# Dealing the forward chain out anew over the sixteen pieces of a segment

## The chip, the cores and the metric

The kernel runs on one core of a Trainium2 chip. The core has a matrix engine (TensorE, PE in the profile, with its weight loads shown as PEld), a vector engine (VectorE, DVE), a scalar engine (ScalarE, ACT), a general engine (GpSimd, POOL) and a sync engine (SyncE, SP), which here only issues DMAs; POOL issues DMAs too. Each engine works through its own list of instructions in order and waits on semaphores for the others. PE writes its products to PSUM, in banks of 512 float32 values per partition; DVE and ACT read them from there.

The metric is the time of one execution in microseconds of device time. The kernel before takes 6149.91 us, the median of three runs (6148.34 to 6164.37).

## The reference

The kernel computes a gated mix of two attention blocks over 2048 tokens of width 576, and all gradients of it. Block A has 32 query heads of width 18 that share one key and one value. Block B is a recurrent transformer: 64 segments of 32 tokens, each with 8 memory tokens in front, 32 heads of width 128; the first 8 rows of a segment's output are the next segment's memory.

```python
for s in range(n_seg):                                   # 64
    xs = x[:, s * seg_len:(s + 1) * seg_len, :].copy()   # 32 tokens
    h = jnp.concatenate([mem, xs], axis=1)               # 8 + 32 rows
    q = jnp.einsum('btd,dhe->bhte', h, Wq)               # k and v in the same way
    scores = jnp.where(mask[None, None], jnp.einsum('bhqe,bhke->bhqk', q, k) * scale, -1000000000.0)
    o = jnp.einsum('bhqk,bhke->bhqe', _softmax(scores), v)
    o = jnp.einsum('bhte,hed->btd', o, Wo)
    mem = o[:, :M, :].copy()                             # 8 rows go on
    outs.append(o[:, M:, :])
...
return g * a + (1 - g) * b       # and the vector-Jacobian product with grad_out
```

So the chain over the segments is serial, with little work in each link: only the 8 memory rows need the link before.

## The kernel before, in words

The program is one long list, unrolled. Its stages are: setup and projections (to about 500 us), the *forward weave* (to about 2330), a bulk stage of block B (to about 3130), a backward weave (to about 4850), and the weight gradients and the end. The change touches the forward weave alone.

`weave` takes two generators and deals their work out by hand, in the order in which it is issued: two steps of the sweep first, then one piece of the chain and one step of the sweep in turn. Nothing reorders this later: each engine's list has the order of the program text.

The *sweep* (`a_pass1`) is block A's attention. Its 1024 steps are 64 blocks (16 pairs of heads, four blocks of 512 queries) of 16 key tiles each. Step n issues, on PE, the score products `a_S` of step n + 1 (two matmuls on separate rows of the array) and the products `a_dP` of step n, then the exponential of step n + 1 on ACT (`a_E`; `a_S` has one buffer), the two multiplications `a_W` on DVE, the accumulation of `a_W` of step n − 1 and of `a_E` of step n into `a_acc` (four matmuls each, one on each quarter of the array's columns). At the end of a block the sum is copied to `acs`, and `a_post` finishes the block in three parts, at steps 2, 3 and 5 of the next one: part 1 transposes `acs` (four float32 transposes into a tile of the buffer `c_pj`, copied to `a_tk` by ACT), part 2 transposes the block's queries from SBUF (four transposes of `a_QD` into `c_pj`, copied to `a_qt` by ACT), part 3 does small work on POOL, ending with the scaling of `a_qt`, and three stores on SP, the last of `a_qt` to `sd_dram`.

The *chain* (`b_chain_fwd`) is block B's memory recurrence. Each segment has 16 pieces, so a segment spans one block of the sweep, and piece p is followed by step p + 2 of the block. A projection works on 32 columns: the 8 memory rows and up to 24 token rows that "ride" along (`load_ride`); its 4096 output columns stand as four column groups of the array times two halves (`proj(w, 0, ...)` and `proj(w, 1, ...)`, each with five contraction tiles of four matmuls of 512 columns). ACT evacuates each half into `c_k2`, `c_q2` or `c_v2`. The chain has two PSUM buffers of one bank each, named `c_pj` and `c_x`; the sweep has six (two for `a_S`, three for `a_dP`, one for `a_acc`). A new tile of `c_pj` or `c_x` waits until the last one has been read.

The pieces of the kernel before, with the names used below:

- 0: the new memory (`pm`, from `hs` and `hx`) goes into `hm`; loads and stores.
- 1 to 4: projection of k, 3, 3, 3 and 1 contraction tiles; 4 to 7: of q (2, 3, 3, 2); 7: transpose of k's memory rows (`mem_T`, `mT_out`).
- 8: transpose of q's memory rows, 2 tiles of v. 9: the scores of the memory queries (`ps`: a mask matmul `mbias` of 128 columns, 32 products with the keys `kx` of the segment, 32 with the memory's keys), and their exponential `c_E`. 10: 3 tiles of v, the row sums `den`, their reciprocal `c_rd` on DVE, the load of the next keys (`load_k`: a transposing DMA from SP into the one buffer `c_kx`). 11 and 12: 3 and 2 tiles of v; 11 also `c_pn` on DVE and its expansion `c_PB` on POOL.
- 13: the output `po` (16 products), the transpose of v's memory rows. 14 and 15: 64 head matmuls of 144 columns each (`heads`: the projection of the memory rows by `Wo`), then `hs` and `hx` on DVE.

`rows_out` (POOL) stores the projected rows, `rows_copy` (SP) copies them within DRAM, `head_out` (SP) stores `c_oh` in runs of 16 bytes, `load_v` loads `c_vx` in four DMAs, and in the first 48 segments `stash` and `stash_end` (SP) transpose two heads of the weights by DMA and store them for a later stage.

Of the kernel before, what the change touches and what calls it, by code (L numbers as in the profile page):

```python
# [6 lines left out]
ACT = mybir.ActivationFunctionType  # L7
# [30 lines left out]
class Kern:  # L38
# [80 lines left out]
    def setup_B_consts(self, pool):  # L119
# [11 lines left out]
        mb = pool.tile([P, P], BF16, name="mbias")  # L131
        nc.gpsimd.memset(mb[:], 0.0)
        nc.gpsimd.memset(mb[:, 64:128], NEGB)
        for c in range(4):
            nc.gpsimd.memset(mb[32 * c:32 * c + 8, 64:128], 0.0)
# [108 lines left out]

    def proj_mem(self, st, Wt, j, psum, tag, nb):
        pj = psum.tile([P, 512], F32, name=tag, bufs=nb)
        self.proj_part(pj, st, Wt, j, range(NKT))
        return pj
# [7 lines left out]
    def b_chain_fwd(self, keep, sp, psum):  # L256
# [50 lines left out]
        for s in range(NSEG):  # L307
# [42 lines left out]
            if s:  # L350
                pm = psum.tile([P, NKT, 8], F32, name="c_x", bufs=1)
# [11 lines left out]
            proj("k", 0, (0, 1, 2), "c_x")  # L363
            yield
            proj("k", 0, (3, 4), "c_x")
            proj("k", 1, (0,), "c_pj")
            yield
            proj("k", 1, (1, 2, 3), "c_pj")
            yield
            proj("k", 1, (4,), "c_pj")  # L370
            proj("q", 0, (0, 1), "c_x")
            yield
            proj("q", 0, (2, 3, 4), "c_x")
            yield
            rows_out("k")
            proj("q", 1, (0, 1, 2), "c_pj")
# [3 lines left out]
            proj("q", 1, (3, 4), "c_pj")  # L380
            mT_out("k", self.mem_T(t2["k"], psum, "c_x", 1))
# [7 lines left out]
            rows_copy("k")  # L389
            ps = psum.tile([P, P], F32, name="c_x", bufs=1)  # L390
            self.mm(ps[:], lhsT=self.identB[:], rhs=self.mbias[:], start=True, stop=False)
            for u in range(8):
                for c in range(4):
                    self.mm(ps[32 * c:32 * c + 32, 8 * u:8 * u + 8], lhsT=kx[:, 8 * c + u, :], rhs=qT[:, u, c, :],
                            start=False, stop=False, tp=(0, 32 * c))
            for u in range(8):
                for c in range(4):
                    self.mm(ps[32 * c:32 * c + 8, 64 + 8 * u:72 + 8 * u], lhsT=mT["k"][:, c, u, :],
                            rhs=qT[:, u, c, :], start=False, stop=True, tp=(0, 32 * c))
            Et = sp.tile([P, 2, 64], BF16, name="c_E", bufs=1)  # L400
            nc.scalar.activation(Et[:].rearrange("p a b -> p (a b)"), ps[:], ACT.Exp, scale=SCALEB)
# [6 lines left out]
            nc.vector.reciprocal(rd[:], den[:])  # L408
# [20 lines left out]
            mT_out("v", self.mem_T(t2["v"], psum, "c_x", 1))  # L429
# [5 lines left out]
            head_out()  # L435
            if not last:
# [980 lines left out]
    def a_pass1(self, keep, sp, psum, xps):  # L1417
# [36 lines left out]
        for n in range(NP_ + 1):  # L1454
# [15 lines left out]
            if n > 0:  # L1470
# [4 lines left out]
                if n % 16 == 0:  # L1475
# [381 lines left out]
```

## Time and profile before

| | us |
|---|---|
| median of three runs | 6149.91 |
| the profiled execution, its own time | 6158.5 |
| its span, first to last instruction | 6156.7 |
| PE busy | 5649.8 (92%) |
| DVE busy | 3760.5 (61%) |
| ACT busy | 3435.7 (56%) |
| POOL busy | 1957.9 (32%) |
| forward weave, first to last exponential `a_E` | 501.4 to 2305.2 |

A line of the timeline has the start, the time that the merged group took, the engine, the line of the kernel (L73 is the helper that issues every matmul, so one goes by tiles there), the operation, what it writes and reads, its shape and the number of instructions; in brackets, how long the engine had been idle before and what released it. "issue" is idle time in which the profile shows nothing to wait for. A line by stretch has busy time and instructions of PE, PEld, DVE, ACT and POOL, then PE's granted clock, the share of the DMA engines and GB/s. Matmuls overlap, so PE's busy time is not its load; the distance between starts is.

### The profile page before, as it was taken

Reading aid. Unit: us, or ns where it says so; the run is one execution under the profiler, and the core shown is the slowest. Engines: PE = TensorE matmul, PEld = TensorE weight load, DVE = VectorE, ACT = ScalarE, POOL = GpSimd, SP = SyncE. Lnnn points to the kernel's source line nnn. Section 1 sums busy time; section 2 is a strip of 40 time slices with the busy share of each in tenths; the row PEclk is TensorE's granted clock in tenths of the full one; section 3 lists DMA queues with packets and bytes.
Section 4 is the critical chain, followed back from the end, with each engine's and each line's share of the span. In section 5 each row is a group of like instructions: output and inputs, shape, how many; then the busy total and the mean of one; then the engine's idle time right before and its main releaser. Section 6 shows DMA issues by size and latency. Waiting matters only on the chain.

```text
span 6156.7 us, 211396 instructions
## 1 busy us (share of the span) xinstructions
PE 5649.8 (92%) x90123; PEld 3274.8 (53%) x90334; DVE 3760.5 (61%) x7124; ACT 3435.7 (56%) x4916; POOL 1957.9 (32%) x3483
## 2 busy tenths in 40 slices
PE   7898999999999996999869999999998999899999
PEld 4543444444444445777735555555555777675444
DVE  4336778777778884666568888888888111111112
ACT  3325777777777774665557777777777222111101
POOL 3002333333333344444423333333333111112213
PEclk7999999999999998999989999999999999999999
DMA  4645666666665548999864443434343999896663
GB/s 151 224 154 115 126 125 130 122 128 126 125 127 115 108 86 231 253 255 254 248 196 109 108 108 109 109 108 108 109 108 98 242 248 246 228 278 200 216 186 112
DMA packets 1369174, 990.03 MB, mean 161 GB/s; under 512 B 931805, under 2 KB 1186790, under 8 KB 1357510
## 3 DMA queue, kind: packets, MB, share of 16 engines
q1 hardware_dynamic: 1286870, 782.63, 51.6%
q0 software_dynamic: 81360, 193.86, 9.8%
q8 instruction: 708, 11.60, 0.8%
q14 instruction: 236, 1.93, 0.1%
HBM read 550.31 MB, written 385.03 MB: 152 GB/s over the span
## 4 chain that ended last, share of the span: by engine, by line
PE 40%; ACT 11%; DMA 6%; issue 3%; SPq 1%; POOL 1%; DVE 0%; POOLq 0%; DVEq 0%; ACTq 0%
ACT b_E L1577 11%; PE w_acc L73 10%; PE b_S L73 6%; PE y_pdx L73 4%; PE r_pj L73 4%; DMA dsx_dram<-x_dS 3%; PE r_x L73 2%; PE x_tr L78 2%; PE b_acc L73 2%; PE y_pk L73 1%; PE x_po L73 1%; PE x_b L73 1%; PE x_m L73 1%; PE b_dP L73 1%; PE f_big L73 1%
## 5 line engine op out<-in xcount | busy, mean ns | idle before, releaser
L1469 DVE TENSOR_TENSOR a_W<-a_dP,a_E 128x512 bf16<-128x512 f32 x2048 | 1316.1, 685 | 357.5 <-issue 133.4
L1598 DVE TENSOR_TENSOR b_dS<-b_dP,b_E 128x512 bf16<-128x512 f32 x2048 | 1313.6, 683 | 240.8 <-issue 121.9
L1577 ACT ACTIVATE b_E<-b_S 128x1024 bf16<-128x1024 f32 x1024 | 1047.8, 1023 | 447.1 <-PE b_dP L73 322.7
L1439 ACT ACTIVATE a_E<-a_S 128x1024 bf16<-128x1024 f32 x1024 | 1049.4, 1025 | 358.0 <-PE a_dP L73 233.9
L73 PE MATMUL b_S<-b_KV,b_QD 32*128 32x512 bf16 x2048 | 400.1, 381 | 158.8 <-ACT b_E L1577 101.6
L73 PE MATMUL r_pj<-WT,r_dT 128*32 128x288 bf16 x12288 | 491.8, 287 | 0.6 <-DMA WT<-st_WT 0.6
L73 PE MATMUL w_acc<-w_d,w_h 128*128 128x512 bf16 (+1 forms) x2352 | 471.0, 379 | 2.5
L73 PE MATMUL a_S<-a_QD,l_KV 32*128 32x512 bf16 x2048 | 401.3, 384 | 39.7 <-ACT a_E L1439 17.9
L73 PE MATMUL b_acc<-b_dS,b_SD 128*32 128x512 bf16 x2048 | 418.7, 390 | 0.9 <-DVE b_dS L1598 0.7
L73 PE MATMUL a_acc<-a_W,l_WK 128*32 128x512 bf16 x4096 | 413.1, 391 | 1.8 <-issue 1.2
L73 PE MATMUL a_acc<-a_E,l_VK 128*32 128x512 bf16 x4096 | 403.8, 383 | 1.8 <-issue 1.8
L73 PE MATMUL b_acc<-b_E,b_SD 128*32 128x512 bf16 x2048 | 403.2, 390 | 0.0
L73 PE MATMUL a_dP<-a_QD,l_KV 32*128 32x512 bf16 x2048 | 399.6, 387 | 0.5 <-issue 0.5
L73 PE MATMUL b_dP<-b_KV,b_QD 32*128 32x512 bf16 x2048 | 398.3, 385 | 0.0
L1063 DVE COPY y_T<-y_pt 128x512 bf16<-128x512 bf16 x256 | 97.1, 420 | 460.2 <-PE y_pt L78 460.2
L73 PEld LDWEIGHTS <-r_dT 128*32 128x32 bf16 x12288 | 332.5, 97 | 79.3 <-issue 1.3
L73 PEld LDWEIGHTS <-w_h 128*128 128x128 bf16 (+1 forms) x2688 | 229.9, 100 | 258.3 <-issue 6.6
L73 PEld LDWEIGHTS <-b_QD 32*128 32x128 bf16 x4096 | 165.0, 91 | 348.5 <-issue 284.3
L73 PEld LDWEIGHTS <-hm 128*32 128x32 bf16 x7680 | 196.8, 96 | 226.0 <-issue 49.9
L73 PEld LDWEIGHTS <-l_KV 32*128 32x128 bf16 x4096 | 129.2, 91 | 300.6 <-issue 264.1
L1049 ACT CAST y_tdk<-y_pk 128x512 bf16<-128x512 f32 x128 | 75.0, 586 | 376.7 <-PE y_pk L73 211.7
L73 PE MATMUL y_pdx<-WT,y_T 128*128 128x288 bf16 x2048 | 273.0, 287 | 0.0
(422 smaller groups left out, 11232.7 us busy)
## 6 DMA issues: line engine op xcount, KB each, us to landing
b_QD<-qd_dram SPq DMA_DIRECT2D x256, 128.0 KB
b_SD<-sd_dram SPq DMA_DIRECT2D x256, 128.0 KB
dOx_dram<-p_tok SPq DMA_DIRECT2D x16, 1024.0 KB
c_vx<-vx_dram SPq DMA_DIRECT2D x256, 64.0 KB
krow_dram<-c_k POOLq DMA_DIRECT2D x64, 256.0 KB
qrow_dram<-c_q POOLq DMA_DIRECT2D x64, 256.0 KB
vrow_dram<-c_v POOLq DMA_DIRECT2D x64, 256.0 KB
x_q<-qx_dram SPq DMA_DIRECT2D x32, 512.0 KB
```

The source lines that it names most:

```text
L73: return self.nc.tensor.matmul(out, lhsT, rhs, start=start, stop=stop, tile_position=tp, skip_group_check=True)
L78: return self.nc.tensor.transpose(out, in_, self.identB[b:b + nrows, b:b + nrows], tile_position=tp)
L1049: nc.scalar.copy(d[w][:, r, :], pk[:])
L1063: nc.vector.tensor_copy(T_[t][w][:], pt[:])
L1439: nc.scalar.activation(E_[n][:], S.pop(n)[:], ACT.Exp, scale=SCALEA)
L1469: nc.vector.tensor_tensor(out=W_[n][:, i, :], in0=dP[i][:], in1=E_[n][:, i, :], op=ALU.mult)
L1577: nc.scalar.activation(E_[n][:], S.pop(n)[:], ACT.Exp, scale=SCALEA)
L1598: nc.vector.tensor_tensor(out=D_[n][:, i, :], in0=dP[i][:], in1=E_[n][:, i, :], op=ALU.mult)
```

## The change

The 16 pieces stay 16, and every product stays, but they are dealt out in another way. The projections of k and q are cut elsewhere (k: 1, 3, 1 + 3, 2 tiles; q: 1, 2, 2 + 1, 4). The second half of v becomes two blocks of 256 columns (`proj_cols`), the first of which shares a tile with the scores and the row sums (`px`, buffer `c_x`); the other has its own (`pv`, buffer `c_pj`) and is copied by DVE. The mask matmul covers 64 columns. `c_pn` and `c_PB` move to the piece of the row sums, the output to piece 12, and the heads to pieces 13 to 15, with 44, 40 and 44 matmuls. In the sweep, `a_qt` comes from DRAM by a transposing DMA on SP in place of PE and ACT, `acs` is transposed into `c_x`, and the parts of `a_post` stand at steps 1, 2 and 5, the first with one transpose and the second with three.

```diff
         self.bmask = bm
-        mb = pool.tile([P, P], BF16, name="mbias")
-        nc.gpsimd.memset(mb[:], 0.0)
-        nc.gpsimd.memset(mb[:, 64:128], NEGB)
+        mb = pool.tile([P, 64], BF16, name="mbias")
+        nc.gpsimd.memset(mb[:], NEGB)
         for c in range(4):
-            nc.gpsimd.memset(mb[32 * c:32 * c + 8, 64:128], 0.0)
+            nc.gpsimd.memset(mb[32 * c:32 * c + 8, :], 0.0)
...
@@ -242,6 +241,12 @@
                         rhs=Wt[:, kt, c * 1024 + j * 512:c * 1024 + (j + 1) * 512],
                         start=(kt == 0), stop=(kt == NKT - 1), tp=(0, 32 * c))
 
+    def proj_cols(self, out, st, Wt, lo, n, kts):
+        for kt in kts:
+            for c in range(4):
+                self.mm(out[32 * c:32 * c + 32, :], lhsT=st[:, kt, :], rhs=Wt[:, kt, c * 1024 + lo:c * 1024 + lo + n],
+                        start=(kt == 0), stop=(kt == NKT - 1), tp=(0, 32 * c))
+
...
         self.proj_part(pj, st, Wt, j, range(NKT))
@@ -348,7 +353,7 @@
             if 0 < s <= 48:
                 stash_end(*wt)
             if s:
-                pm = psum.tile([P, NKT, 8], F32, name="c_x", bufs=1)
+                pm = psum.tile([P, NKT, 8], F32, name="c_pj", bufs=1)
...
                 self.mm(pm[0:64, 4, :], lhsT=hx[:].rearrange("p g c -> p (g c)"), rhs=self.sel8[:])
@@ -360,25 +365,27 @@
             nc.gpsimd.dma_start(self.pq_dram[s // 4].rearrange("s q c w k -> (s q c) w k")
                                 [:, 4 * (s % 4):4 * (s % 4) + 4, :], self.zeros[:].unsqueeze(1).to_broadcast([P, 4, P]))
             yield
-            proj("k", 0, (0, 1, 2), "c_x")
-            yield
-            proj("k", 0, (3, 4), "c_x")
-            proj("k", 1, (0,), "c_pj")
-            yield
-            proj("k", 1, (1, 2, 3), "c_pj")
-            yield
-            proj("k", 1, (4,), "c_pj")
-            proj("q", 0, (0, 1), "c_x")
-            yield
-            proj("q", 0, (2, 3, 4), "c_x")
-            yield
+            proj("k", 0, (0,), "c_pj")
+            yield
+            proj("k", 0, (1, 2, 3), "c_pj")
+            yield
+            proj("k", 0, (4,), "c_pj")
+            proj("k", 1, (0, 1, 2), "c_x")
+            yield
+            proj("k", 1, (3, 4), "c_x")
+            proj("q", 0, (0,), "c_pj")
+            yield
+            mT_out("k", self.mem_T(t2["k"], psum, "c_x", 1))
             rows_out("k")
-            proj("q", 1, (0, 1, 2), "c_pj")
+            proj("q", 0, (1, 2), "c_pj")
+            yield
+            proj("q", 0, (3, 4), "c_pj")
+            proj("q", 1, (0,), "c_x")
             if s < 48:
                 wt = stash(2 * s)
             yield
-            proj("q", 1, (3, 4), "c_pj")
-            mT_out("k", self.mem_T(t2["k"], psum, "c_x", 1))
+            proj("q", 1, (1, 2, 3, 4), "c_x")
+            rows_copy("k")
             yield
             src = self.mem_T(t2["q"], psum, "c_x", 1)
             qT = sp.tile([P, 8, 4, 8], BF16, name="c_qT", bufs=1)
@@ -386,39 +393,46 @@
             rows_out("q")
             proj("v", 0, (0, 1), "c_pj")
             yield
-            rows_copy("k")
-            ps = psum.tile([P, P], F32, name="c_x", bufs=1)
-            self.mm(ps[:], lhsT=self.identB[:], rhs=self.mbias[:], start=True, stop=False)
+            px = psum.tile([P, 512], F32, name="c_x", bufs=1)
+            ps, den = px[:, 0:P], px[:, P:192]
+            for c in range(4):
+                self.mm(px[32 * c:32 * c + 32, 64:128], lhsT=self.identB[:, 32 * c:32 * c + 32],
+                        rhs=self.mbias[:], start=True, stop=False, tp=(0, 32 * c))
             for u in range(8):
                 for c in range(4):
-                    self.mm(ps[32 * c:32 * c + 32, 8 * u:8 * u + 8], lhsT=kx[:, 8 * c + u, :], rhs=qT[:, u, c, :],
-                            start=False, stop=False, tp=(0, 32 * c))
+                    self.mm(px[32 * c:32 * c + 32, 8 * u:8 * u + 8], lhsT=kx[:, 8 * c + u, :], rhs=qT[:, u, c, :],
+                            tp=(0, 32 * c))
             for u in range(8):
                 for c in range(4):
-                    self.mm(ps[32 * c:32 * c + 8, 64 + 8 * u:72 + 8 * u], lhsT=mT["k"][:, c, u, :],
+                    self.mm(px[32 * c:32 * c + 8, 64 + 8 * u:72 + 8 * u], lhsT=mT["k"][:, c, u, :],
                             rhs=qT[:, u, c, :], start=False, stop=True, tp=(0, 32 * c))
             Et = sp.tile([P, 2, 64], BF16, name="c_E", bufs=1)
-            nc.scalar.activation(Et[:].rearrange("p a b -> p (a b)"), ps[:], ACT.Exp, scale=SCALEB)
-            yield
-            proj("v", 0, (2, 3, 4), "c_pj")
-            den = psum.tile([P, 64], F32, name="c_x", bufs=1)
-            self.mm(den[:], lhsT=self.blockones[:], rhs=Et[:, 0, :], start=True, stop=False)
-            self.mm(den[:], lhsT=self.blockones[:], rhs=Et[:, 1, :], start=False, stop=True)
+            nc.scalar.activation(Et[:].rearrange("p a b -> p (a b)"), ps, ACT.Exp, scale=SCALEB)
+            proj("v", 0, (2, 3), "c_pj")
+            yield
+            proj("v", 0, (4,), "c_pj")
+            self.mm(den, lhsT=self.blockones[:], rhs=Et[:, 0, :], start=True, stop=False)
+            self.mm(den, lhsT=self.blockones[:], rhs=Et[:, 1, :], start=False, stop=True)
             rd = sp.tile([P, 64], F32, name="c_rd", bufs=1)
-            nc.vector.reciprocal(rd[:], den[:])
-            if not last:
-                kx = load_k(s + 1)
-            yield
-            proj("v", 1, (0, 1, 2), "c_x")
+            nc.vector.reciprocal(rd[:], den)
             pn = sp.tile([P, 2, 64], BF16, name="c_pn", bufs=1)
             nc.vector.tensor_tensor(out=pn[:], in0=Et[:], in1=rd[:].unsqueeze(1).to_broadcast([P, 2, 64]), op=ALU.mult)
             PB = sp.tile([P, 16, 4, 8], BF16, name="c_PB", bufs=1)
             self.expand(PB[:], pn[:].rearrange("p a (u q) -> p (a u) q", q=8), 16)
             nc.gpsimd.dma_start(self.pm_dram[s], pn[:].rearrange("p a b -> p (a b)"))
-            yield
+            if not last:
+                kx = load_k(s + 1)
+            vlo = px[:, 256:512]
+            self.proj_cols(vlo, h_, self.W["v"], 512, 256, (0, 1, 2))
+            yield
+            self.proj_cols(vlo, h_, self.W["v"], 512, 256, (3, 4))
+            nc.scalar.copy(t2["v"][:, 4:6, :].rearrange("p u e -> p (u e)"), vlo)
+            pv = psum.tile([P, 512], F32, name="c_pj", bufs=1)
+            self.proj_cols(pv[:, 0:256], h_, self.W["v"], 768, 256, range(NKT))
+            nc.vector.tensor_copy(t2["v"][:, 6:8, :].rearrange("p u e -> p (u e)"), pv[:, 0:256])
             rows_copy("q")
-            proj("v", 1, (3, 4), "c_x")
-            yield
+            yield
+            mT_out("v", self.mem_T(t2["v"], psum, "c_x", 1))
             po = psum.tile([P, 8, 32], F32, name="c_pj", bufs=1)
             for u in range(8):
                 self.mm(po[:, u, :], lhsT=vx[:, u, :], rhs=PB[:, u].rearrange("p c q -> p (c q)"), start=True, stop=False)
@@ -426,24 +440,26 @@
                         start=False, stop=True)
             oT = sp.tile([P, 8, 4, 8], BF16, name="c_oT", bufs=2)
             nc.vector.tensor_copy(oT[:].rearrange("p u c q -> p u (c q)"), po[:])
-            mT_out("v", self.mem_T(t2["v"], psum, "c_x", 1))
             rows_out("v")
             nc.gpsimd.dma_start(self.oTm_dram[s // 16][:, s % 16, :], oT[:].rearrange("p u c q -> p (u c q)"))
             oh = sp.tile([P, 4, 8, 8], BF16, name="c_oh", bufs=1)
             nc.gpsimd.tensor_copy(oh[:], oT[:].rearrange("p u c q -> p c u q"))
             yield
-            head_out()
             if not last:
                 vx = load_v(s + 1)
                 if s < 48:
                     stash_end(*wt)
                     wt = stash(2 * s + 1)
                 ph = psum.tile([P, 512], F32, name="c_pj", bufs=1)
-                heads(0, 16)
+                heads(0, 11)
+            yield
+            head_out()
+            if not last:
+                heads(11, 21)
             yield
             rows_copy("v")
             if not last:
-                heads(16, 32)
+                heads(21, 32)
                 hs = sp.tile([P, P], BF16, name="c_hs", bufs=1)
                 nc.vector.tensor_copy(hs[:], ph[:, 0:P])
                 hx = sp.tile([P, 4, 16], BF16, name="c_hx", bufs=1)
@@ -1476,10 +1492,11 @@
                     acs = sp.tile([P, 512], F32, name="a_acs", bufs=1)
                     nc.scalar.copy(acs[:], acc[:])
                     bb = n // 16 - 1
-                    post = self.a_post(bb // 4, bb % 4, acs, QD.pop(bb), sp, xps, dl_all)
+                    QD.pop(bb)
+                    post = self.a_post(bb // 4, bb % 4, acs, sp, xps, dl_all)
             if n < NP_ and n % 16:
                 acc_mm(acc, n, E_, self.VK, False, False)
-            if post is not None and n % 16 in (2, 3, 5):
+            if post is not None and n % 16 in (1, 2, 5):
                 if next(post, "end") == "end":
                     post = None
             yield
@@ -1495,21 +1512,19 @@
         nc.gpsimd.dma_start(self.qd_dram[:].rearrange("p (a r) t -> p a r t", r=32)[:, 2:4, 18:20, :],
                             self.dl_dram[:].rearrange("(p a r) t -> p a r t", a=2, r=2))
 
-    def a_post(self, p, qb, acs, QD, sp, psum, dl_all):
-        nc = self.nc
-        pt = psum.tile([P, 4, P], F32, name="c_pj", bufs=1)
+    def a_post(self, p, qb, acs, sp, psum, dl_all):
+        nc = self.nc
+        qt = sp.tile([P, 4, 4, 32], BF16, name="a_qt", bufs=1)
+        nc.sync.dma_start_transpose(qt[:].rearrange("p a b c -> p a (b c)"), self.qd_dram[p][:, qb * 512:(qb + 1) * 512])
+        pt = psum.tile([P, 4, P], F32, name="c_x", bufs=1)
         for j in range(4):
             nc.tensor.transpose(pt[:, j, :], acs[:, j * P:(j + 1) * P], self.identF[:])
+            if j == 0:
+                yield
         tk = sp.tile([P, 4, 2, 64], F32, name="a_tk", bufs=1)
         tkf = tk[:].rearrange("p a b c -> p (a b c)")
         ptf = pt[:].rearrange("p a b -> p (a b)")
         nc.scalar.copy(tkf, ptf)
-        yield
-        pd = psum.tile([P, 4, P], BF16, name="c_pj", bufs=1)
-        for j in range(4):
-            self.tr(pd[:, j, :], QD[:, j * P:(j + 1) * P], P)
-        qt = sp.tile([P, 4, 4, 32], BF16, name="a_qt", bufs=1)
-        nc.scalar.copy(qt[:].rearrange("p a b c -> p (a b c)"), pd[:].rearrange("p a b -> p (a b)"))
         yield
         rl = sp.tile([P, 4, 2, 2], F32, name="a_rl", bufs=2)
         nc.vector.reciprocal(rl[:, :, 1, :], tk[:, :, :, 18])
```

More of the change, by code (lines that the diff above doesn't have):

```diff
@@ L362, in b_chain_fwd @@
             yield
-            proj("k", 0, (0, 1, 2), "c_x")
+            proj("k", 0, (0,), "c_pj")
             yield
-            proj("k", 0, (3, 4), "c_x")
-            proj("k", 1, (0,), "c_pj")
+            proj("k", 0, (1, 2, 3), "c_pj")
             yield
-            proj("k", 1, (1, 2, 3), "c_pj")
+            proj("k", 0, (4,), "c_pj")
+            proj("k", 1, (0, 1, 2), "c_x")
             yield
-            proj("k", 1, (4,), "c_pj")
-            proj("q", 0, (0, 1), "c_x")
+            proj("k", 1, (3, 4), "c_x")
+            proj("q", 0, (0,), "c_pj")
             yield
-            proj("q", 0, (2, 3, 4), "c_x")
+            mT_out("k", self.mem_T(t2["k"], psum, "c_x", 1))
+            rows_out("k")
+            proj("q", 0, (1, 2), "c_pj")
             yield
-            rows_out("k")
-            proj("q", 1, (0, 1, 2), "c_pj")
+            proj("q", 0, (3, 4), "c_pj")
+            proj("q", 1, (0,), "c_x")
             if s < 48:
```

## The prediction

> **What bounds the kernel now.** I read the busy times by stretch first. The edits lie in one stretch, the forward weave from about 500 to 2305 us (1805 us), where PE is nearly always busy and its granted clock is 1.00:
>
> ```profile
> 530.00:2300.00 1770.00, 1701.59 (x35172) 759.63 (x35168) 1419.05 (x2586) 1368.67 (x1765) 676.76 (x1387) 1.00 0.61 121
> ```
>
> Then the timeline of one segment. A *period* is the time from the `a_S` pair before a chain piece to the pair after it. This is piece 5, twelve projection matmuls:
>
> ```profile
> 1200.18 0.39 PE L73 MATMUL a_S<-a_QD,l_KV 32*128 32x512 bf16 x2 [0.24 <-ACT a_E L1439]
> ...
> 1200.51 0.40 PE L73 MATMUL a_acc<-a_W,l_WK 128*32 128x512 bf16 x4
> ...
> 1200.66 1.02 ACT L1439 ACTIVATE a_E<-a_S 128x1024 bf16<-128x1024 f32 x1
> ...
> 1200.74 0.39 PE L73 MATMUL a_acc<-a_E,l_VK 128*32 128x512 bf16 x4
> ...
> 1200.95 0.82 PE L73 MATMUL c_x<-Wq,hm 128*32 128x512 bf16 x12
> ...
> 1201.73 0.39 PE L73 MATMUL a_S<-a_QD,l_KV 32*128 32x512 bf16 x2
> ```
>
> Two limits meet here. *Floor*: the next pair waits for the exponential that reads the one PSUM buffer of S: 0.48 from pair to exponential, 1.02 for it, 0.05 back, 1.55 us. *PE sum*: 0.55 to the second accumulation group, 0.21 to the chain's first matmul, 0.64 for twelve projection matmuls (0.213 per contraction tile), 0.12 to the next pair: 1.53. A piece up to twelve projection matmuls costs the floor; what it has beyond costs time one for one.
>
> From the starts of the `a_S` pairs, the median periods 0 to 15 over the 64 segments are 1.55, 2.22, 2.36, 1.55, 1.55, 1.55, 1.65, 1.60, 1.72, 1.62, 1.69, 1.55, 1.55, 1.57, 1.87, 1.66: sum 27.28. The mean sum is 28.22, so 0.94 per segment (60 us) lies in outliers. Period 2 is long through a wait, and the list of waits has it 63 times:
>
> ```profile
> 1224.64 0.40 PE L78 MATMUL c_pj<-identB,a_QD 128*128 128x128 bf16 x4
> ...
> 1225.17 0.58 ACT L1512 COPY a_qt<-c_pj 128x512 bf16<-128x512 bf16 x1
> ...
> 1225.80 0.40 PE L73 MATMUL c_pj<-Wk,hm 128*32 128x512 bf16 x4 [0.21 <-ACT a_qt L1512]
> ```
>
> The outliers sit in periods 14, 15 and the next 0, where PE stops inside the head products though nothing they read is late:
>
> ```profile
> 1212.19 1.63 SPq L281 DMA_TRANSPOSE c_kx<-kx_dram  x1
> ...
> 1217.52 0.39 PE L73 MATMUL c_pj<-WoN,c_oT 128*8 128x144 bf16 x12 [1.07 <-issue]
> ```
>
> They follow the k transpose. Where SP issued `c_kx` under 3 us before the pair that ends period 13 (16 segments), periods 14, 15 and 0 exceed their medians by 1.77 us a segment; 3 to 4 us before (20), by 0.49; earlier (27), by 0.19. In all 43 us. The transpose's packets end about 4.4 us after issue, so it hurts when it runs into the heads, which start 0.77 after that pair.
>
> **The change, period by period.** The medians first, by the PE sum.
> - 0: one float32 transpose of `acs` (four with their switch take 0.59 at 1222.42) fits in PE's slack of about 0.14 there: 1.55.
> - 1: 12 projection matmuls become 4, four float32 transposes three: 0.76 + 0.11 + 0.46 + 0.21 + 0.12 = 1.66. Period 15 shrinks, so the copies `hs`, `hx` (0.29, 0.21) run behind a later `a_W` and delay the next one by 0.17: 1.83 (before 2.22).
> - 2: the bf16 transposes, the `a_qt` copy and the wait go: 1.55 (2.36).
> - 3 and 7: 16 projection matmuls: 0.76 + 0.85 + 0.12 = 1.75 each (1.55, 1.60).
> - 4 and 6: twelve, their evacuation (0.58) mid-piece: 1.55. 5: a memory transpose and 8 matmuls, as period 8 before: 1.72. 8: unchanged, 1.72.
> - 9: the mask matmul shrinks from 0.32 with its switch to about 0.05 (64 columns on four column tiles); key products 0.20 and memory products 0.30, new 8 projection matmuls 0.43: 0.76 + 0.05 + 0.20 + 0.30 + 0.43 + 0.12 = 1.86 (1.62).
> - 10: below, 2.86 (1.69).
> - 11: `vlo` tiles 3, 4 and `pv`, together 3.5 full tiles (256-column ones at half of 0.213: four head matmuls of 144 columns take 0.061, the same rate per column): 1.63 (1.55).
> - 12: the 16 output products and the transpose of v, as period 13 before, plus 0.01: 1.58. 13 and 14: 44 and 40 head matmuls at 0.0152 (64 take 0.98): sums 1.56 and 1.50, to which the `c_oT` copy, now behind `a_W`, adds 0.02 and 0.16: 1.58, 1.66 (1.57, 1.87). 15: no second accumulation group: floor, 1.55 (1.66).
>
> **Period 10.** `den` (scores' columns 128 to 191) and `vlo` (256 to 511) now share one tile, and so one PSUM bank. The vector engine reads `den`, then PE is to write `vlo`. That two engines do not overlap in one bank on other columns is seen in the last stage: `f_ptr` is evacuated in two column ranges, by ACT and DVE, and DVE waits for ACT although its transposes were done before 6085.4.
>
> ```profile
> 6087.95 0.58 ACT L70 COPY f_T<-f_ptr 128x512 bf16<-128x512 bf16 x1 [2.53 <-PE f_big L73]
> ...
> 6088.56 0.22 DVE L68 COPY f_T<-f_ptr 64x128 bf16<-64x128 bf16 x1 [1.27 <-ACT f_T L70]
> ```
>
> The reciprocal is queued on DVE behind the period's two multiplies:
>
> ```profile
> 1208.33 0.39 PE L73 MATMUL a_S<-a_QD,l_KV 32*128 32x512 bf16 x2
> ...
> 1208.85 1.29 DVE L1469 TENSOR_TENSOR a_W<-a_dP,a_E 128x512 bf16<-128x512 f32 x2 [0.33 <-ACT c_E L401]
> ...
> 1210.12 0.56 DVE L408 RECIPROCAL c_rd<-c_x 128x64 f32<-128x64 f32 x1
> ```
>
> So it ends 2.35 after the pair. PE is done with `den` at about 1.25 and has `vlo` next; behind `vlo` stand the next S pair, the exponential and all of the sweep. `vlo` starts at 2.40, takes 0.32, and 0.12 later comes the pair: 2.86. Without the wait it is 0.76 + 0.21 + 0.27 + 0.32 + 0.12 = 1.68. I take 2.86: the bank row is the nearest. Its cover would be none, as nothing else is queued on PE.
>
> In the Trainium skill, "PSUM — Partial Sum Buffer", section "PSUM bank collisions raise a hardware error", speaks against the change too: guard by bank and quadrant, not by address. By that rule the wait stands (+1.18 here), by columns it would be nothing.
>
> Sum after 27.69, against 27.28: +0.41, times 64 = +26 us.
>
> **Queues.** On POOL the stores of k's transpose and rows move from pieces 7 and 6 to 5, `pm` and `c_PB` from 11 to 10, v's stores and the `c_oh` copy from 13 to 12 (0.54 each, `c_PB` 1.07); on SP `rows_copy` of k moves from 9 to 7, of q from 12 to 11. POOL is busy 38% and none of these is read within the segment but `c_PB`. SP gains a transpose of q per block (issue 1.2 to 1.6, as `c_wt` and `c_kx`), behind `rows_copy("v")`, which now takes the blockage after the `c_oh` store that `c_vx` takes today (four issues took 7.65 at 1218.19; 4.4 to 4.8 in the two other segments I followed). `load_v` and the weight stash move ahead of that store. POOL must wait for the transpose before it scales `a_qt`, and its `sd` store, the k-row store and `rows_copy("k")` queue behind. Following SP from the pair before `load_v`: 1.8 loads, 3.9 stash, 0.6 store, 4.5 blockage, 1.3 v rows, 1.3 transpose, 1.5 small, 3.5 `dq` and `sd` with the wait, 2.7 stash and wait, 1.3 k rows, 0.6 load: `c_kx` some 23 us after, 5 before the pair ahead of the heads, lead 5.8 us. Today the median in the 48 stash segments is 3.3 plus 0.77. At that lead the rows above charge 0.2 a segment or less: 43 falls to about 10, −33 us. Bounds: 0 if the lead doesn't grow; more than today's if it falls under 3.8. `c_PB` on POOL has about 5 us of slack to its product in period 12, so the q transpose can be that late for nothing.
>
> "DMA: Bandwidth & Descriptors", section "Queues, rings and completion order", has each engine take turns between queues packet by packet. By that, a transpose holds up no other queue for microseconds and this gain would be 0; then the sum is +26. The segments counted above disagree.
>
> DMA share in the stage is 0.61; the q transpose (128 KB) adds about what one stash does (two add 0.18, 0.64 against 0.46): nothing waits on share. Masks, `a_QD` reads that end earlier and the last block's tail: about 0, at most 2 us.
>
> **Sum.** +26 − 33 = −7 us. The profiled execution took 6158.5 (span 6156.7 and 1.8 around it), 8.6 above the median of 6149.9; taken to the median: 6143. No change, then, by the 0.3% (18 us) that a measurement of this kernel can tell.
>
> **Rivals.**
> - *The bank wait does not come.* Period 10 is 1.68, but reciprocal, `c_pn` (0.28) and the copy of `pv` (0.42) then crowd DVE and delay its multiplies, which gives back 0.30 in period 12: −0.88 × 64 = −56: 6143 − 56 = 6087. For it: PE's columns are disjoint. Against: the `f_T` row.
> - *The k transpose still meets the heads*, because POOL's wait for q delays the k rows as much as the new order gains. The stalls stay at 43: 6150 + 26 = 6176, slower. It decides from a lead of 4.8 us or less.
> - *The queue falls further behind*: lead under 3.8 in the stash segments: 1.77 × 48 = 85 in place of 43: 6176 + 42 = 6218. For it: SP is given one more transpose and one more wait on POOL. Against: `load_v` no longer stands behind the store.
> - *The change gives nothing*: the wait of period 2 moves to period 1 or 3. Against: `c_x` is free two periods before k needs it. It ends near the first sum.
>
> **How the numbers follow.** Forecast 0.48 (6125 to 6168: ±13 for the sixteen sums, ±16 for the stalls); no bank wait 0.13; stalls stay 0.20; queue behind 0.11; others 0.08. Faster by over 0.3% (under 6131): 0.13 + 0.07 + 0.05 = 0.25. Slower (over 6168): 0.17 + 0.11 + 0.06 + 0.04 = 0.38. Same 0.37. Range 6085 to 6192: leaves out the queue case and tails.
>
> **What would show it.** Right: median periods 2 at 1.55 and 10 at 2.8 to 2.9, with PE waiting for `c_rd` in each segment; waits of `c_pj` on `a_qt` gone; few "issue" stops in the heads, `c_kx` issued over 5 us ahead of them. Wrong: period 10 under 1.8; `c_PB` or `a_qt` at the head of a PE wait; `issue` stops as many as the 29 now.

## The result, and the profile after

The changed kernel takes 6197.36 us, the median of four runs (6196.02 to 6198.67), against 6157.14 for the kernel before on the same chip (four runs, 6148.34 to 6168.74): a ratio of 1.0064, 95% interval [1.0044, 1.0085]. It is slower, by 40 us where 7 us less was forecast, and outside the predicted range. All later ratios are to the kernel before on their own chip, where it took 6164 to 6174.

The profiled execution has a span of 6193.8 us, 37.1 more than before. The forward weave, from the first to the last exponential, takes 1856.5 us in place of 1803.9: 52.6 more. The rest of the program is 15 us shorter. The edits do not touch it, and over the eighteen kernels profiled here it lies between 4337 us (the changed kernel) and 4359, so I do not count this as the change's.

In the stretch from 530 to 2300 us PE is less busy than before (1641.9 in place of 1701.6 us), though the stage is longer:

```profile
530.00:2300.00 1770.00, 1641.88 (x35260) 754.30 (x35263) 1406.17 (x2571) 1282.97 (x1653) 660.49 (x1346) 0.99 0.65 123
```

Most of that is no saving: over its whole weave PE is busy 1718 us here and was 1728 before. So little work went, and waits came. PE's list of waits in the same stretch names them: line and tile, what was waited for, microseconds in all, times, the longest.

```profile
PE c_x L73 <- DVE c_rd L417: 65.4, 62, 2.4
PE c_pj L73 <- issue: 21.6, 24, 2.0
PE a_acc L73 <- issue: 9.8, 11, 3.3
PE a_S L73 <- ACT a_E L1455: 8.6, 22, 0.6
PE c_x L73 <- issue: 3.9, 8, 1.2
PE a_dP L73 <- issue: 3.1, 2, 2.4
```

In the same list of the kernel before stand:

```profile
PE c_pj L73 <- issue: 21.0, 29, 1.9
PE c_pj L73 <- ACT a_qt L1512: 14.0, 63, 0.5
```

The wait of period 2 for `a_qt` is gone. The first line of the list after is new, one wait in each segment: period 10, the bank. In the timeline of one segment PE has finished `den`, and starts `vlo` only when DVE's reciprocal has ended:

```profile
1168.89 0.39 PE L73 MATMUL a_S<-a_QD,l_KV 32*128 32x512 bf16 x2
...
1169.66 0.58 PE L73 MATMUL c_pj<-Wv,hm 128*32 128x512 bf16 x4
1170.17 0.23 PE L73 MATMUL c_x<-c_E,blockones 128*128 128x64 bf16 x2
1171.58 0.51 PE L73 MATMUL c_x<-Wv,hm 128*32 128x256 bf16 x12 [1.18 <-DVE c_rd L417]
1172.02 0.39 PE L73 MATMUL a_S<-a_QD,l_KV 32*128 32x512 bf16 x2
```

```profile
1169.77 1.29 DVE L1485 TENSOR_TENSOR a_W<-a_dP,a_E 128x512 bf16<-128x512 f32 x2 [1.42 <-issue]
1170.98 0.55 DVE L417 RECIPROCAL c_rd<-c_x 128x64 f32<-128x64 f32 x1
```

The median periods 0 to 15 are 1.64, 1.68, 1.55, 1.74, 1.55, 1.72, 1.55, 1.74, 1.72, 1.88, 2.77, 1.64, 1.57, 1.56, 1.55, 1.55: sum 27.41, where before it was 27.28 and 27.69 was forecast. Times 64 that is +8 us. What remains of the 52.6 are outliers. I call *outliers* what the periods exceed their medians by, summed over the stage: 59.5 us before, 103.5 after (+44). For them a period is counted from the start of one exponential to that of the next (there is one behind each `a_S` pair) and set against the medians of these. In the segments with a weight stash after the first they are 86.5 us (47.8 before): 14.7 in period 9, 10.2 in 10, 6.3 in 11, 40 in 12 to 15 (before: 1.1, 0, 0.3 and 38), the rest mostly in 0 to 2 (14; before 8); in the 16 without a stash 6.5. So the growth lies in periods 9 to 11, +30 us, and hardly in the heads.

Two such stops. In the first, SP issues the queries' transpose; its packets ran from 1314.39 to 1317.48, the next block of PE's instructions was fetched from 1317.28 to 1318.44, and PE, which waits for no engine, goes on 1.35 us after that:

```profile
1311.86 1.21 SPq L1518 DMA_TRANSPOSE a_qt<-qd_dram  x1
1313.18 0.52 SPq L303 DMA_DIRECT2D st_WT<-c_wt  x1
```

```profile
1317.18 0.62 PE L73 MATMUL c_pj<-Wv,hm 128*32 128x512 bf16 x7
1319.79 0.38 PE L73 MATMUL c_pj<-Wv,hm 128*32 128x512 bf16 x1 [1.99 <-issue]
```

The second is the old one, the keys' transpose (issued at 884.32) inside the heads. Its packets ran from 885.67 to 889.13; here the fetch had begun just ahead of them, at 885.63, and landed at 887.17, and PE goes on 1.76 us after that:

```profile
887.25 0.80 PE L73 MATMUL c_pj<-WoN,c_oT 128*8 128x144 bf16 x39
888.93 0.23 PE L73 MATMUL c_pj<-WoN,c_oT 128*8 128x144 bf16 x1 [0.88 <-issue]
```

`c_kx` is issued 0.46 us (median of the stash segments) before the pair ahead of the heads, where 5 was forecast and 3.32 was the value before; in 18 of 47 segments it is issued after that pair.

### The profile page after: what moved, and what is told of

Read it like the earlier page. It is cut to its first block, busy times and chain, and to the rows that moved or that the text cites. A ratio compares the mean times of both kernels' runs of the same rounds, so it can differ in the third digit from the quotient of the medians.

```text
span 6193.8 us, 214086 instructions
## 1 busy us (share of the span) xinstructions
PE 5635.6 (91%) x91339; PEld 3289.3 (53%) x91550; DVE 3789.4 (61%) x7188; ACT 3388.1 (55%) x4852; POOL 1960.8 (32%) x3482
## 4 chain that ended last, share of the span: by engine, by line
PE 38%; ACT 11%; DMA 5%; issue 5%; SPq 1%; POOL 1%; DVE 0%; POOLq 0%; DVEq 0%; ACTq 0%
ACT b_E L1592 11%; PE w_acc L73 10%; PE b_S L73 6%; PE r_pj L73 4%; PE y_pdx L73 3%; DMA dsx_dram<-x_dS 3%; PE r_x L73 2%; PE x_tr L78 2%; PE b_acc L73 2%; PE x_b L73 1%; PE x_po L73 1%; PE y_pk L73 1%; PE x_m L73 1%; PE f_big L73 1%; PE b_dP L73 1%
## 5 line engine op out<-in xcount | busy, mean ns | idle before, releaser
L73 PEld LDWEIGHTS <-hm 128*32 128x32 bf16 x8960 | 227.5, 97 | 246.5 <-issue 85.9
```

What stands on the lines that cost most here:

```text
L73: return self.nc.tensor.matmul(out, lhsT, rhs, start=start, stop=stop, tile_position=tp, skip_group_check=True)
```

## The experiments

The table gives, for each, the ratio with its interval, the sum of the median periods, the outliers and the length of the weave in its profiled execution. The medians are those between pairs, the outliers those between exponentials; where stops are many the two do not add up to the weave. Counted between pairs the outliers are 206 in kernel 1, 98 in 5, 216 in 9, 188 in 10, 113 in 11, 165 in 12, and at most about 6 us more than in the table elsewhere.

| kernel | ratio | medians | outliers | weave |
|---|---|---|---|---|
| before | 1 | 27.28 | 59.5 | 1803.9 |
| changed | 1.0064 [1.0044, 1.0085] | 27.41 | 103.5 | 1856.5 |
| 1 own piece | 1.0133 [1.0105, 1.0161] | 26.59 | 202 | 1905.7 |
| 2 q by PE | 1.0024 [1.0010, 1.0037] | 27.89 | 41 | 1827.3 |
| 3 q early | 0.9989 [0.9977, 1.0001] | 27.41 | 59 | 1817.2 |
| 4 old deal, q by DMA | 1.0302 [1.0281, 1.0324] | 31.25 | in the medians | 2018.5 |
| 5 DMA unread | 1.0104 [1.0070, 1.0137] | 27.83 | 90 | 1877.9 |
| 6 = 1 + 3 | 0.9950 [0.9933, 0.9967] | 26.58 | 89 | 1795.3 |
| 7 = 1 + 2 | 0.9954 [0.9938, 0.9969] | 26.99 | 60 | 1785.9 |
| 8 old deal, q early | 0.9982 [0.9966, 0.9999] | 27.46 | 64 | 1819.5 |
| 9 stores on POOL | 1.0300 [1.0274, 1.0327] | 27.60 | 199 | 1981.7 |
| 10 = 6 + 9 | 1.0128 [1.0092, 1.0163] | 26.65 | 168 | 1892.4 |
| 11 = 7 + 9 | 1.0033 [1.0019, 1.0047] | 27.04 | 96 | 1841.5 |
| 12 `c_oh` on POOL | 1.0199 [1.0176, 1.0222] | 27.69 | 153 | 1936.0 |
| 13 plain copy unread | 1.0033 [1.0019, 1.0047] | 27.85 | 48 | 1834.3 |
| 14 before, k early | 0.9946 [0.9930, 0.9961] | 27.26 | 35 | 1778.7 |
| 15 changed, k early | 1.0021 [1.0011, 1.0030] | 27.39 | 76 | 1827.5 |
| 16 = 7, k early | 0.9902 [0.9886, 0.9917] | 26.96 | 27 | 1751.2 |

### 1 to 4: the parts, one at a time

**1.** `vlo` begins in piece 11, when the reciprocal is done, so the shared bank costs nothing:

```diff
             vlo = px[:, 256:512]
-            self.proj_cols(vlo, h_, self.W["v"], 512, 256, (0, 1, 2))
             yield
-            self.proj_cols(vlo, h_, self.W["v"], 512, 256, (3, 4))
+            self.proj_cols(vlo, h_, self.W["v"], 512, 256, range(NKT))
```

> All of the vlo products go into piece 11, behind one step of the sweep; the shared tile, and all else, stays. Theory A (the bank wait is paid in full, 1.08 us of PE in each period 10): period 10 falls from 2.77 to the floor of 1.55 and period 11 rises from 1.64 to about 1.96, -0.90 a segment, -58 us, so about 6140, with the wait of c_x on c_rd gone and the outliers above the medians at about 100 us as in the changed kernel. Rival (the wait is only a place where time is lost that another engine would lose anyway): within 10 us of the changed kernel, 6190 to 6205.

The wait went (period 10 is 1.55) and the medians gave 53 us, but the kernel became slower than the changed one, by 43 us, which neither expectation had. The waits of PE:

```profile
PE c_pj L73 <- issue: 36.4, 29, 4.3
PE a_S L73 <- ACT a_E L1454: 30.9, 70, 2.5
PE c_pj L73 <- POOL c_PB L221: 27.4, 23, 3.1
PE c_x L73 <- issue: 19.8, 18, 2.5
PE a_acc L73 <- issue: 14.7, 14, 2.4
```

With PE quicker through the segment, the same queue work comes later in it: `c_kx` is issued 1.9 us behind the pair ahead of the heads (0.46 ahead of it in the changed kernel), and POOL waits 336 us for the queries (209), so that `c_PB` is late too.

**2.** The queries are transposed by PE and copied by ACT again, at step 3 into `c_x`. **3.** They stay with the DMA, but it is issued at step 6 of its own block, into a second buffer, eleven steps before it stood:

```diff
+                if kt == 6:
+                    b = n // 16
+                    QT[b] = sp.tile([P, 4, 4, 32], BF16, name="a_qt", bufs=2)
+                    nc.sync.dma_start_transpose(QT[b][:].rearrange("p a b c -> p a (b c)"),
+                                                self.qd_dram[b // 4][:, b % 4 * 512:(b % 4 + 1) * 512])
```

> Only the q transpose by DMA is undone: PE transposes the queries again, now into c_x at step 3 of the block, where nothing waits for that buffer. Medians: period 2 from 1.55 to about 1.9, +21 us. Theory B (the transposing DMA of q, by its place in SP's queue or by its load, makes the stops of PE): outliers fall from about 104 us to 50 or less, sum about 6165 to 6175. Rival C (the new pieces are too dense in PE instructions, whatever the DMA queues do): outliers stay at about 100, so about 6218.

> The q transpose by DMA stays, but is issued about nine steps earlier, at step 6 of its own block, into a second buffer; POOL then waits for nothing from SP. Theory B1 (place: SP's queue behind the c_oh store, and POOL's wait for it): outliers fall from about 104 us to 50 or less, about 6145 to 6155. Rival B2 (load: a third and fourth transposing DMA per segment in flight, wherever it is issued): outliers stay at 90 to 100, 6185 to 6200. Rival C (dense pieces): the same as B2.

Either takes the growth away: outliers 41 and 59. So the 44 us came with the transposing DMA in the place that the change gave it. There its packets took 3.4 us from first to last (median), in kernel 3 about 2.1.

**4.** The kernel before with only its queries by that DMA, at steps 2 and 5.

> The kernel before with one part of the change: q by transposing DMA, issued when the block's sum is copied, in place of the four PE transposes and the ACT copy; the old dealing of pieces stays. Medians: period 2 from 2.36 to 1.55, -52 us. Theory B (the q DMA makes the stops): outliers grow from about 60 us by 30 to 45, so 6140 to 6155 against 6157. Rival C (dense new pieces make them): outliers stay at about 60, so about 6105.

Much dearer than thought, and in another way: POOL waits for the queries, and `c_PB` stands behind that wait on POOL (the first line is POOL's, the second PE's). Periods 13 and 14 become 4.86 and 3.26.

```profile
POOL a_qt L1535 <- DMA a_qt<-qd_dram: 494.0, 53, 13.2
...
PE c_pj L73 <- POOL c_PB L222: 177.3, 46, 6.9
```

### 5 to 8: POOL's wait, or the transfer itself?

**5.** Queries by PE as in 2, but the transposing DMA is still issued in its place:

```diff
+        qu = sp.tile([P, 4, P], BF16, name="a_qu", bufs=1)
+        nc.sync.dma_start_transpose(qu[:], self.qd_dram[p][:, qb * 512:(qb + 1) * 512])
         pt = psum.tile([P, 4, P], F32, name="c_x", bufs=1)
```

> The queries are transposed by PE again, as in the second run, but the transposing DMA of the changed kernel is still issued in its place, into a buffer that nothing reads. The DMA's packets and SP's issue time are there, POOL's wait for them is not. If it is POOL's in-order wait that costs (209 us of waiting in the changed kernel, 0 with the queries by PE), this takes the time of the second run: 1.002 to 1.004 of the kernel before, outliers above the medians 30 to 50 us. If the packets themselves or SP's issue of them cost, it takes that and the 59 us by which the changed kernel's early outliers exceed the second run's: 1.010 to 1.013.

Nobody reads the result, and it costs 0.8% against 2 (49 us; outliers 90 for 41). My theory that POOL's wait was the cost fell for the changed kernel: the transfer costs by itself. Of its outliers 25 us lie in period 9 (1 in kernel 2).

**6, 7** put 1 together with 3 and with 2. **8** is the kernel before with 3.

> Both the own piece for the first half of v's last columns (period 10 without its wait: the medians' sum 26.59 in place of 27.41) and the early transpose of the queries. If the own piece lost time only because POOL's wait for the queries then bites (336 us of it, c_PB late for PE 23 times), the wait is 0 here and the gain of 0.82 x 64 = 52 us shows: 0.989 to 0.992 of the kernel before. If PE's pause in period 10 sheltered the queues whatever the queries do, the outliers grow from about 59 us to 110 or more and the time is 0.997 to 1.006.

> The own piece with the queries transposed by PE: medians' sum 27.06 (27.89 less 0.83). If the own piece only lost to POOL's wait: the second run's time less 50 us, 0.993 to 0.996 of the kernel before. If PE's pause was a shelter: outliers above 80 us where the second run has 41, and 1.000 to 1.005.

> The kernel before with one thing changed: its queries come by the transposing DMA, issued at step 6 of their own block into a second buffer. Period 2 loses the PE transposes and the wait for their copy: 2.36 to 1.55, x 64 = 52 us; POOL waits for nothing new. If the place of the transpose is what counts: 0.990 to 0.993 of the kernel before, with the outliers as before (59 us). If one more transpose per block costs by itself, wherever it stands: its outliers grow by the 40 us that the changed kernel's do and it ends at 0.997 to 1.000. If POOL still waits for it: above 1.01.

So the own piece, worth 53 us by the medians, gives 43 us with the queries by PE (7 against 2), 24 with the early DMA (6 against 3) and costs 43 with the DMA in its first place (1 against the changed kernel). Kernel 8 gained 11 of the 52 us expected: period 2 fell to 1.55, but period 1 rose from 2.22 to 3.21, since the list of SP comes so late that PE waits for the riding rows (`c_x` for `hm`, 57.7 us, 35 times).

### 9 to 12: making SP's list shorter

If SP's list is late, fewer entries should help. **9 to 11** issue the three stores at the end of `a_post` from POOL, **12** the store of `c_oh`:

```diff
-        nc.sync.dma_start(otd(self.otok_dram), ot[:].rearrange("p a b c -> p a (b c)"))
+        nc.gpsimd.dma_start(otd(self.otok_dram), ot[:].rearrange("p a b c -> p a (b c)"))
```

> The changed kernel with the three stores at the end of a block (attention output, its gradient rows, scaled queries) issued by POOL, which computes them, in place of SP. SP then no longer waits for POOL or for the transposed queries. Theory Q, SP's list is nearly full (per stash segment of 29.3 us it issues for 19.8 us, waits 6.3 us for transfers and only 3.8 us for other engines; before it was 18.0, 5.3 and 9.1): SP's waits for engines rise to 6 us or more, the outliers fall from 103 to 45 to 65 us, and the time is 0.998 to 1.001 of the kernel before. Rival P, the packets of the queries' transpose stop PE where they lie, however free SP is: outliers stay near 100 us, 1.005 to 1.008.

> Own piece and early transpose of the queries, with the same three stores on POOL. Theory Q: outliers from 89 to 50 to 60 us at medians of 26.58, so 0.989 to 0.991 of the kernel before. Rival P: as without it, 0.994 to 0.996. If POOL's issue of the stores makes its list late for PE, slower than that, with PE waiting for c_PB.

> Own piece and the queries by PE, with the same three stores on POOL. Here SP waits 5.8 us a segment for engines already and the outliers are 60 us: by theory Q they fall to 45 us at most, 0.992 to 0.994; by rival P nothing is gained, 0.995.

> The changed kernel with the one store of c_oh, 4096 runs of 16 bytes, issued by POOL in place of SP. If what is late for the queries' transpose is that it stands behind those 4096 packets in SP's ring (its packets then take 3.4 us where the early one takes 2.2), its landing comes some 3 us earlier, POOL's wait for it (209 us) falls to under 100 us and the outliers from 103 to 60 us: 0.999 to 1.002. If SP's own list of issues is what is late, SP is 0.7 us a segment freer and little changes: 1.004 to 1.007. If POOL takes microseconds to issue 4096 runs, c_PB comes late and it is slower than the changed kernel.

All four lost, 0.8 to 2.4% against their own base. In kernel 9 SP did issue less (18.0 us a segment for 19.8), but it spends the rest waiting for transfers. SP's waits in the changed kernel:

```profile
SPq L299 <- DMA st_WT<-c_wt: 149.4, 52, 4.9
SPq L328 <- DMA krow_dram<-c_k: 125.9, 61, 4.4
```

and in kernel 9:

```profile
SPq L299 <- DMA st_WT<-c_wt: 407.7, 95, 8.8
SPq L328 <- DMA krow_dram<-c_k: 278.1, 56, 14.1
```

The store of k's rows now stands behind the three others on POOL, SP waits for it, and behind SP stands `c_kx`: SP issues it in piece 10 in kernel 2, in 12 in the changed one and in 13 here (medians). In kernel 12 the cost is another: `c_PB` is late on POOL, and PE waits for it 82.8 us (31 times; 1.3 us in the changed kernel). What is late is a chain of transfers through two queues, and an entry moved from one to the other only changes its place in the chain.

### 13 to 16: what in the transfer costs

In the traces the instruction fetches of PE (a queue of their own, 16 KB each, one per 6.5 us) start less often while a transposing DMA has packets in flight, and bunch at its end. Counted over the stash segments (expected: the mean rate of fetches times the time looked at):

```
                    fetches started in flight   within 0.8 us of the end of it
                    counted   expected          counted   expected
before                  7        36                44        18
changed                23        62                52        23
all 18 kernels        404       871               827       366
```

The transposing DMAs move 256 bytes a packet. Small packets alone do not give this picture: counted in the same way over all 18 kernels for the store of `c_oh`, 4096 packets of 16 bytes, fewer fetches start in flight too (361, expected 512), but none bunch at its end (72, expected 101).

So theory F: PE runs out of instructions because the transpose holds up the fetch of the next block, and does so where it takes instructions fastest, in the heads (40 to 44 short matmuls a piece) and in piece 9 (64 of 8 columns). Rival L: any entry makes SP late. **13** is kernel 5 with a plain copy of the same bytes:

```diff
-        qu = sp.tile([P, 4, P], BF16, name="a_qu", bufs=1)
-        nc.sync.dma_start_transpose(qu[:], self.qd_dram[p][:, qb * 512:(qb + 1) * 512])
+        qu = sp.tile([P, 512], BF16, name="a_qu", bufs=1)
+        nc.sync.dma_start(qu[:], self.qd_dram[p][:, qb * 512:(qb + 1) * 512])
```

**14 to 16** issue the other transpose, that of the keys, in piece 4 into a second buffer, on the kernel before, the changed one and kernel 7 (`c_oT` has one buffer in place of two, to make room):

```diff
-            kx = sp.tile([P, HB, 32], BF16, name="c_kx", bufs=1)
+            kx = sp.tile([P, HB, 32], BF16, name="c_kx", bufs=2)
...
             proj("k", 1, (3, 4), "c_x")
             proj("q", 0, (0,), "c_pj")
+            if not last:
+                kxn = load_k(s + 1)
...
-                kx = load_k(s + 1)
+                kx = kxn
```

> As the fifth run (queries by PE, a DMA of the block's queries from DRAM into a buffer that nothing reads), but the DMA is a plain copy of the same 128 KB in place of the transposing one. Theory F, the transposing packets hold up PE's instruction fetches: no cost, the second run's 1.001 to 1.004 of the kernel before, outliers about 41 us. Theory L, any further DMA at that place in SP's list costs: 1.008 to 1.013, as with the transpose.

> The kernel before with one change: the transposing load of the next keys has two buffers and is issued in piece 4, among projections, in place of piece 10 (one other tile, c_oT, has one buffer in place of two to make room). SP issues the same list. Theory F: the stops of PE in the heads (38 of the 48 us of early outliers lie in periods 13 to 15) go for the most part, since projections take instructions half as fast: 0.993 to 0.996 of the kernel before. Theory L: nothing is gained, 0.999 to 1.001.

> The same edit on the changed kernel. Theory F: of its early outliers of 86 us the 40 in periods 12 to 15 fall to about 10; those of periods 9 to 11, which go with the queries' transpose, stay: 0.999 to 1.003 of the kernel before. Theory L: as the changed kernel, 1.004 to 1.008.

> The same edit on the changed deal with its own piece for the columns of v and with the queries transposed by PE (0.9954 of the kernel before without it). Theory F: its 37 us in periods 12 to 15 fall to 10, 0.989 to 0.992. Theory L: 0.994 to 0.997.

All four ratios came out as F had it. The plain copy costs 0.1% against kernel 2 where the transpose cost 0.8%, and of outliers periods 9 to 11 have 1 us in kernel 2, 2 with the plain copy and 35 with the transpose. In the heads L keeps a part: `c_kx` is issued 2.7 us ahead of the pair in kernel 5, 3.6 in 13 and in 2. PE's waits with the transpose unread (5):

```profile
PE c_pj L73 <- issue: 25.2, 31, 1.8
PE c_x L73 <- issue: 17.1, 19, 2.2
```

and with the plain copy (13), where no `c_x` wait on "issue" is in the list:

```profile
PE c_pj L73 <- issue: 13.5, 17, 1.7
PE a_S L73 <- issue: 1.4, 3, 0.9
```

In 15 the outliers of periods 12 to 15 fall from 40 to 17 us (10 was expected); those of 9 to 11, which go with the queries, do not fall (43 for 31). The place in the program text is not the time at which it runs: SP, late with its list, issues the piece-4 transpose in piece 11, 10 and 8 (medians of 14, 15 and 16), 4.1, 5.1 and 8.6 us ahead of the pair in place of 3.3, 0.5 and 2.4. That is enough: its packets run on into the heads in 19, 9 and 0 of 47 segments, where it was 34 in the kernel before and 45 in the changed one. Kernel 16 is 1.0% faster than the kernel before and 1.6% faster than the changed one: medians 26.96, outliers 27; of stops on "issue" this is left from 530 to 2200 us:

```profile
PE c_pj L73 <- issue: 6.8, 15, 1.1
PE a_acc L73 <- issue: 0.7, 1, 0.7
PE a_S L73 <- issue: 0.6, 2, 0.4
```

## Why the prediction was wrong, by its steps

- **The medians** (+26 forecast, +8 measured). Right in kind everywhere: floor in periods 2, 4 and 6, the two pieces of 16 matmuls at 1.74, period 5 and 8 at 1.72, 9 at 1.88 (1.86 forecast). The bank wait came, 62 times and 65.4 us, period 10 at 2.77 (2.86, though the terms written for it add to 2.84). The section "PSUM bank collisions raise a hardware error" of the Trainium skill's "PSUM — Partial Sum Buffer", to guard by bank and quadrant and not by address, fits these waits, which are on a semaphore of the program; no run here left the guard out. Mis-sized were the small delays that I charged: period 1 at 1.68 in place of 1.83, 14 at 1.55 in place of 1.66, so the late `c_oT` and `hs` copies cost nothing; period 0 was dearer, 1.64 in place of 1.55.
- **The queues** (−33 forecast, +44 measured) is the step that failed: "`c_kx` some 23 us after, 5 before the pair". The path fell short at both ends. From the first `c_vx` load to `c_kx` SP takes 26.1 us (median) in place of 23, 21.3 in the kernel before. And I let the loads start at the pair; they start 2.3 us behind it, since the late `c_kx` and the rows of q stand ahead of them. That makes 28.4 of a segment of 29. SP's list closes on itself: what it is late by at the end of a segment it is late by at the start of the next. Per segment of 29.3 us it issues for 19.8 and waits 6.3 for transfers; only 3.8 are waits for other engines, 9.1 before (part of the waits lies inside the issues: before, the three add to 32.4 us of a segment of 28.3). With the queries by PE (2) the lead is 3.6 us, so the queries' transpose costs 3.1 of it.
- The second part of that step: I had taken the queries' transpose as load on SP alone. That it "adds about what one stash does: nothing waits on share" was right about share (0.65 for 0.61), and beside the point: runs 5 and 13 show that the transpose costs PE time though nothing waits for it, and a plain copy hardly does, which no step of mine charged; I had the rule for the keys and didn't apply it to the queries. Periods 9 to 11 had no term for it, and grew by 30 us.
- The rival "the queue falls further behind" had the lead right, and its total is near: it gave 42 us more of stalls and 6218; measured were 44 more of outliers, and the medians 18 us cheaper than in its sum. But it put those 42 us into the heads and the next period 0. In the stash segments after the first, periods 12 to 15 and 0 to 2 together went from 46 us to 54 only; the rest came in 9 to 11, so its total is luck. Kernel 15 has about the lead that I forecast, 5.1 us, and there these periods have 18 us, 28 less than before: the gain forecast for that lead (33) was about right, and the lead was wrong.
- "DMA: Bandwidth & Descriptors", "Queues, rings and completion order", has the engines take turns between queues packet by packet, and was read as saying that a transpose holds up no other queue for microseconds. Run 13 against 5 and the count of fetches speak against that reading in this case: 404 fetches started in flight where the mean rate gives 871.
- The signs that I named told it: `issue` stops stayed (47 in the list after, 36 before), and `c_kx` was not 5 us ahead.

## What to carry to other kernels

A list of DMAs that one engine issues in a loop has to be added up around the loop: if its issue time and its waits for transfers come near the period (here 19.8 and 6.3 of 29.3 us), a further entry is paid by what stands behind, and a quicker matrix engine can make it worse (kernel 1). A transposing DMA belongs where the matrix engine takes few instructions, well ahead of runs of short matmuls. Its time has to be read from the trace, not from its place in the program: "issue" stops of PE in the list of waits, set against the time of each transpose, show where it stands now. A wait that is taken away (the bank, 53 us by the medians) is worth that only if the queues can keep the new pace.

## What was not expected of the hardware

- A transposing DMA of 128 KB whose result nobody reads costs the matrix engine 49 us in 64 segments, a plain copy of the same bytes 6 (by the ratios to kernel 2; their intervals leave about ±22 and ±12). In kernel 5, PE goes on 1.2 to 1.75 us after the last fetch has landed in 28 of its 37 "issue" stops of over 0.6 us. That the late fetch is what stops PE fits this and the counts, but no run changed the fetches alone, and which part of the chip the two share was not tried.
- The packets of the queries' transpose take about 2.1 us from first to last in one place of the program and 3.4 to 4.0 in another, beside copies of rows within DRAM. That the longer flight is why the first place costs more fits these runs but is only argued.
- Three stores of 36, 36 and 128 KB, moved from SP to POOL, cost 2.4% of the program in the changed kernel, 1.8% in kernel 6 and 0.8% in kernel 7.
